# Later-block transposes of a two-layer MLP moved from TensorE to 32x32 transposes on VectorE

## Chip, cores, metric

The kernel runs on one core of one Trainium2 chip. The metric is the device time of one execution in microseconds (us). Before the change it is 411.44 us (median of 4 runs, 411.21 to 412.17). The profile's span leaves out about 1.7 us of that. Engines are named as in the profile: PE is the matmul engine and PEld its weight loads, DVE is VectorE, ACT ScalarE, POOL GpSimd, SP the engine that issues DMAs.

## The reference

```python
B, S, D, F = 1, 2048, 1024, 3584          # all bf16
def reference(x, w1, b1, w2, b2):
    y = _layernorm(x, axis=-1)             # no scale, no shift, eps 1e-5
    h = gelu_tanh(jnp.einsum("bsd,df->bsf", y, w1) + b1)
    return jnp.einsum("bsf,fd->bsd", h, w2) + b2
```

## The kernel before

The 2048 rows are 16 tiles of 128 rows, in four blocks of 512. All weights stay in SBUF. For each block PE computes hT = gelu(w1.T y.T + b1) in 28 groups of 8 matmuls ("first matmul", L509), then the output in 8 groups of 28 matmuls of 512 columns ("second matmul", L527). One output group is 6.04 us of PE.

The first matmul contracts over D, so it needs y transposed, with D on partitions. Each normalized 128x1024 tile is turned by eight PE transposes of 128x128 into PSUM, and another engine copies the result into `yT`. For blocks 1 to 3 these batches of eight stand between the first four output groups of the block before:

```python
def phase2(b):                                   # PE
    for st in range(TPB):
        for dc in range(NDC):
            bank = O_BANKS[n_o % len(O_BANKS)]   # two output banks
            w.wait(s_oe, n_o - len(O_BANKS) + 1) # the bank was evacuated
            for k in range(KF):
                ...                              # 28 matmuls of 512 columns
            ins.then_inc(s_o, 1)
            n_o += 1
            q = st * NDC + dc
            if b + 1 < NB and q < TPB:
                transposes((b + 1) * TPB + q)    # 8 PE transposes of the next block
```

ACT copies those twelve tiles to `yT`, and DVE evacuates the output banks, adding b2:

```python
# ACT, after the gelus of block b
for t in range((b + 1) * TPB, (b + 2) * TPB):
    for ui in tile_units[t]:
        copy_unit(ui)                            # yT <- PSUM, 128x1024

# DVE
for b in range(NB):
    if b + 1 < NB:
        for t in ...: stats_of(t)                # mean and variance
        for t in ...: normalize(t)               # waits for POOL's 1/sqrt of that tile
    evacs(b)                                     # 8 evacuations of 128x512
```

At the start, tile 0's reciprocal root is done on DVE (a chain of dependent one-column instructions) and every other tile's on POOL. The DVE order is: statistics, normalize and copy tile 0; statistics of 1 and of 2; normalize and copy 1; then statistics of 3, tile 2, tile 3. PE's order in block 0 comes from a small planner in the kernel that models when data arrive. It cuts the first groups into narrow pieces of 128, 256 or 384 columns, so that PE can begin with one tile.

Of the kernel before, what the change touches and what calls it, by code (L numbers as in the profile page):

```python
# [11 lines left out]
P = 128  # L12
LN_EPS = 1e-5
# [3 lines left out]
N_WARM = 0  # L17


class _Eng:  # L20
# [5 lines left out]
    def wait(self, sem, val):  # L26
        if val <= 0:
            return
        if self.seen.get(sem.name, 0) >= val:
            return  # L30
        self.seen[sem.name] = val
        self.e.wait_ge(sem, val)
# [15 lines left out]
def _plan_block0(KF, TPB, avail_ft, t_norm, t_pe0, c_tr, c_copy, c_col):  # L48
# [6 lines left out]
    while n_done < KF * TPB:  # L55
        if next_tr < TPB and t_norm[next_tr] <= t:
            ops.append(("T", next_tr))
            t += c_tr
            ready[next_tr] = t + c_copy
            next_tr += 1  # L60
            continue
# [15 lines left out]
        if best is not None:  # L77
            i, j0, j1 = best
            ops.append(("G", i, j0, j1))
            for j in range(j0, j1):  # L80
                done[i][j] = True
            n_done += j1 - j0
            t += c_col * (j1 - j0)
            continue
# [7 lines left out]
def bass_standalone__mixer_channel_mlp__prompt_kernel(nc, x, w1, b1, w2, b2, out):  # L92
# [27 lines left out]
    dma_order = [("x", 0), ("b1", 0), ("x", 1) if TPB > 1 else None]  # L120
    nx = 2
# [6 lines left out]
    while nx < TPB:  # L128
        dma_order.append(("x", nx))
        nx += 1  # L130
# [9 lines left out]
    dma_order = [d for d in dma_order if d is not None]  # L140

    def dma_bytes_rate(kind, idx):
        if kind == "x":
            return P * D * 2, 0.387
        if kind == "b1":
            return F * 2, 0.05
        if kind == "b2":
            return P * D * 2, 0.387
        if kind == "w1":
            a, b = w1_chunks[idx]  # L150
            by = (b - a) * P * D * 2
            desc = (b - a) * P * 2
            return by, (0.290 if desc <= 512 else 0.348 if desc <= 1024 else 0.387)
        a, b = w2_chunks[idx]
        return (b - a) * P * D * 2, 0.387

    t = 2.75
    arrive = {}
    for kind, idx in dma_order:
        by, rate = dma_bytes_rate(kind, idx)  # L160
        t += by / 1024.0 / 1024.0 * 1.048576 / rate / 1000.0 * 1000.0 / 1000.0 if False else by / (rate * 1e6)
        arrive[(kind, idx)] = t + 0.6
    avail_ft = [arrive[("w1", ft_chunk[ft])] for ft in range(KF)]
    DVE_CHAIN_TILES = [0]
    dve_b0 = [("S", 0), ("N", 0), ("C", 0)]
    for j in range(1, TPB):
        dve_b0.append(("S", j))
        if j + 1 < TPB and j == 1:
            dve_b0.append(("S", j + 1))
        if j >= 2 and j + 1 < TPB:  # L170
            dve_b0.append(("S", j + 1))
        dve_b0.append(("N", j))
        dve_b0.append(("C", j))
    seen_ops = set()
    dve_b0 = [o for o in dve_b0 if not (o in seen_ops or seen_ops.add(o))]
    c_stats, c_chain_v, c_chain_p, c_norm, c_tr, c_copy = 1.7, 1.9, 3.2, 0.6, 0.5, 0.8
# [4 lines left out]
    for kind, j in dve_b0:  # L181
        if kind == "S":
            tv = max(tv, arrive[("x", j)]) + c_stats
            if j not in DVE_CHAIN_TILES:
                tp_chain = max(tp_chain, tv) + c_chain_p
                rs_done[j] = tp_chain
        elif kind == "N":
            if j in DVE_CHAIN_TILES:
                tv += c_chain_v
            else:  # L190
                tv = max(tv, rs_done[j])
            tv += c_norm
            t_norm[j] = tv
        else:
            tv = max(tv, t_norm[j] + c_tr) + c_copy
    plan, _t_end = _plan_block0(KF, TPB, avail_ft, t_norm, t_norm[0], c_tr, c_copy, 0.45)
    assert plan[0] == ("T", 0)

    units = [(0, 0, KH, T_BANKS[0], "V"), (0, KH, KD, T_BANKS[1], "V")]
    for tt in range(1, NT):  # L200
        units.append((tt, 0, KD, T_BANKS[len(units) % 2], "V" if tt < TPB else "A"))
    cnt = {"V": 0, "A": 0}
    unit_copy_count = []
    for (_t0, _a, _b, _bank, cp) in units:
        cnt[cp] += 1
        unit_copy_count.append((cp, cnt[cp]))
# [12 lines left out]
    for b in range(1, NB):  # L219
        for ft in range(KF):  # L220
            groups.append((b, ft, 0, SB))
            for j in range(TPB):
                h_need[(b, ft, j)] = len(groups)

    with ExitStack() as es:
# [39 lines left out]
        s_ca = E(nc.semaphore("s_ca"))  # L265
# [8 lines left out]
        s_copy = {"V": s_cv, "A": s_ca}  # L274
# [6 lines left out]
        def _(sp):  # L281
# [14 lines left out]
            n_out = 0  # L296
            for b in range(NB):
                for st in range(TPB):
                    t = b * TPB + st
                    last = (b == NB - 1 and st == TPB - 1)  # L300
                    if not last:
                        w.wait(s_oe, (t + 1) * NDC)
                        sp.dma_start(out[0, t * P:(t + 1) * P, :], x_sb[:, t, :]).then_inc(s_od, 16)
                        n_out += 1
                    else:
                        for dc in range(NDC):
                            w.wait(s_oe, t * NDC + dc + 1)
                            sp.dma_start(out[0, t * P:(t + 1) * P, dc * DC:(dc + 1) * DC],
                                         x_sb[:, t, dc * DC:(dc + 1) * DC]).then_inc(s_od, 16)
                            n_out += 1  # L310
            sp.wait_ge(s_od, 16 * n_out)
# [20 lines left out]

        POOL_CHAIN_TILES = [t for t in range(NT) if t not in DVE_CHAIN_TILES]
        pool_rs_count = {t: i + 1 for i, t in enumerate(POOL_CHAIN_TILES)}
        pool_st_count = {t: i + 1 for i, t in enumerate(POOL_CHAIN_TILES)}

        RSTD_FIN = (NR_ITERS - 1) % 2

        @block.gpsimd
        def _(g):  # L340
# [7 lines left out]
            for t in POOL_CHAIN_TILES:  # L348
                w.wait(s_st, pool_st_count[t])
# [3 lines left out]
        def _(v):  # L353
            w = _Eng(v)
            nv = 0

            def chain(ins):
                nonlocal nv
                nv += 1
                ins.then_inc(s_v, 1)  # L360
                w.wait(s_v, nv)

            n_st = [0]

            def stats_of(t):
# [4 lines left out]
                if t in DVE_CHAIN_TILES:  # L370
                    chain(ins)
                else:
                    ins.then_inc(s_st, 1)
                    n_st[0] += 1
                    assert pool_st_count[t] == n_st[0]

            cnt_v = [0]

            def normalize(t):
                if t in DVE_CHAIN_TILES:  # L380
                    nonlocal nv
                    cnt_v[0] = nv
                    last = rstd_single(v, w, t, s_v, cnt_v)
                    nv = cnt_v[0]
                    chain(last)
                else:
                    w.wait(s_rs, pool_rs_count[t])
                v.tensor_scalar(x_sb[:, t, :], x_sb[:, t, :], mv[:, t, 0:1], ry[:, RSTD_FIN, t:t + 1],  # L388
                                ALU.subtract, ALU.mult).then_inc(s_y, 1)

            def copy_unit(ui):
                t, k0, k1, bank, cp = units[ui]
                assert cp == "V"
                slot = (t // TPB) % NYS
                j = t % TPB
                w.wait(s_tr, ui + 1)
                v.tensor_copy(yT[:, k0:k1, slot * SB + j * P: slot * SB + (j + 1) * P],  # L397
                              ps_t(bank)[:, k0:k1, :]).then_inc(s_cv, 1)

            def copies(t):  # L400
                for ui in tile_units[t]:
                    copy_unit(ui)

            def evacs(b):
                for st in range(TPB):
                    t = b * TPB + st
                    for dc in range(NDC):
                        n_ev = t * NDC + dc
                        bank = O_BANKS[n_ev % len(O_BANKS)]
                        w.wait(s_b2, 16)  # L410
                        w.wait(s_o, n_ev + 1)
                        v.tensor_tensor(x_sb[:, t, dc * DC:(dc + 1) * DC], ps[:, bank, 0:DC],  # L412
                                        b2_bc[:, dc * DC:(dc + 1) * DC], ALU.add).then_inc(s_oe, 1)

            for kind, j in dve_b0:
                if kind == "S":
                    stats_of(j)
                elif kind == "N":
                    normalize(j)
                else:  # L420
                    copies(j)
            for b in range(NB):
                if b + 1 < NB:
                    for t in range((b + 1) * TPB, (b + 2) * TPB):
                        stats_of(t)
                    for t in range((b + 1) * TPB, (b + 2) * TPB):
                        normalize(t)
                evacs(b)

        @block.scalar  # L430
        def _(a):
# [6 lines left out]

            def copy_unit(ui):
                t, k0, k1, bank, cp = units[ui]  # L440
                assert cp == "A"
                slot = (t // TPB) % NYS
                j = t % TPB
                w.wait(s_tr, ui + 1)
                a.activation(yT[:, k0:k1, slot * SB + j * P: slot * SB + (j + 1) * P],  # L445
                             ps_t(bank)[:, k0:k1, :], ACTF.Copy).then_inc(s_ca, 1)

            gi = 0
            for b in range(NB):
                while gi < len(groups) and groups[gi][0] == b:  # L450
# [126 lines left out]
```

## Time and profile before

| part | us | where read |
|---|---|---|
| time, span | 411.44, 409.8 | runs, page |
| PE busy | 397.8 (97%) | page |
| DVE, ACT, POOL busy | 59.1, 94.9, 38.1 | page |
| second matmul of block 0, with transposes | 50.14 | chain of waits |
| the same in the last block, without | 48.36 | chain of waits |
| one batch of 8 PE transposes | 0.45 | chain of waits |

From the page of the kernel before, its first line of busy time, then the shares of the chain that ended last:

```profile
PE 397.8 (97%) x2041; PEld 192.9 (47%) x2041; DVE 59.1 (14%) x110; ACT 94.9 (23%) x142; POOL 38.1 (9%) x142
...
PE 95%; DMA 2%; SPq 1%; DVE 1%; issue 0%
PE ps L527 47%; PE ps L509 46%; PE ps L482 2%; DMA x_sb<-in_x_dram 2%; SPq L292 1%; DVE stats L368 0%; SPq L285 0%; DVE yT L397 0%; DVE x_sb L412 0%; SPq L287 0%; DVE x_sb L388 0%; DVE mv L369 0%
```

The chain is PE's own work: two matmul lines hold 93%, and the transposes (L482) hold 2%. A faster DVE, ACT or POOL would shorten nothing in the middle of this kernel.

The chain of waits in order of time for the same kernel (start, duration, what):

```profile
63.13 6.04 PE ps L527 x28
69.17 0.45 PE ps L482 x8
69.62 6.04 PE ps L527 x28
75.67 0.45 PE ps L482 x8
...
88.64 0.45 PE ps L482 x8
89.09 24.17 PE ps L527 x112
```

Each batch of eight transposes pushes the following output group back by 0.45 us. The last four groups (24.17 us) have none between them.

The start, from the timeline of PE, with the idle time before a piece and what ended it in brackets:

```profile
8.17 1.04 PE L482 MATMUL ps<-ident,x_sb 128*128 128x128 bf16 x8 [4.25 <-DVE x_sb L388]
9.38 5.85 PE L509 MATMUL ps<-yT,w_sb 128*128 128x128 bf16 x64 [0.18 <-DVE yT L397]
15.35 0.62 PE L482 MATMUL ps<-ident,x_sb 128*128 128x128 bf16 x8
```

Tile 0 is transposed at 8.17, eight narrow groups (64 matmuls of 128 columns) run to 15.23, and tile 1 is transposed at 15.35. In this run nothing seems to separate the groups from the transposes. That reading turns out to matter, the more so as the chain of waits of the same profile goes another way there: not through the groups, but through the arrival of tile 2's x, its statistics and the normalization of tile 1, which ends at 15.30.

```profile
6.86 6.33 DMA x_sb<-in_x_dram
...
14.88 0.42 DVE x_sb L388
15.30 0.05 issue
15.35 0.64 PE ps L482 x8
```

The end, from the chain of waits: the last evacuation takes 0.69 us, and the span ends at 409.8, so 2.16 us of store follow.

```profile
406.95 0.69 DVE x_sb L412
```

### The profile page before, as it was taken

The numbers are of one execution on the slowest core, as the hardware profiler recorded it, in microseconds if no ns is written. First come the engines' busy times: TensorE is split into PE (matmuls) and PEld (weight loads), VectorE is DVE, ScalarE is ACT, GpSimd is POOL, SyncE is SP. The second block draws the span as 40 slices with busy tenths as digits, with TensorE's granted clock in tenths as the row PEclk, the third lists the DMA queues.
The fourth block names the chain that finished last, engine by engine and source line by source line (L and its number), as shares of the span: only waits on it lengthen the run. The fifth ranks groups of instructions, "written<-read, shape, count | busy, mean of one in ns | idle before, by whom it ended". The sixth has DMA issues, their size and how long they took to land.

```text
span 409.8 us, 4576 instructions
## 1 busy us (share of the span) xinstructions
PE 397.8 (97%) x2041; PEld 192.9 (47%) x2041; DVE 59.1 (14%) x110; ACT 94.9 (23%) x142; POOL 38.1 (9%) x142
## 2 busy tenths in 40 slices
PE   2999999999999999999999999999999999999997
PEld 1854475454444444444444444445444444444443
DVE  5526100011071000011034000011010000001101
ACT  1434342120034433021004444221002333300000
POOL 0606300000054000000007100000000000000000
PEclk9999999999999999999999999999999999999999
DMA  8999940000000000000000000000000000000000
GB/s 231 346 361 386 387 163 2 27 26 2 26 26 2 0 0 2 0 27 26 26 27 0 2 0 0 2 26 2 26 26 27 0 0 2 0 2 26 26 27 26
DMA packets 18014, 23.63 MB, mean 58 GB/s; under 512 B 843, under 2 KB 10315, under 8 KB 17995
## 3 DMA queue, kind: packets, MB, share of 16 engines
q1 hardware_dynamic: 17994, 23.34, 16.8%
q8 instruction: 16, 0.26, 0.3%
q14 instruction: 4, 0.02, 0.0%
HBM read 19.14 MB, written 4.19 MB: 57 GB/s over the span
## 4 chain that ended last, share of the span: by engine, by line
PE 95%; DMA 2%; SPq 1%; DVE 1%; issue 0%
PE ps L527 47%; PE ps L509 46%; PE ps L482 2%; DMA x_sb<-in_x_dram 2%; SPq L292 1%; DVE stats L368 0%; SPq L285 0%; DVE yT L397 0%; DVE x_sb L412 0%; SPq L287 0%; DVE x_sb L388 0%; DVE mv L369 0%
## 5 line engine op out<-in xcount | busy, mean ns | idle before, releaser
L509 PE MATMUL ps<-yT,w_sb 128*128 128x512 bf16 (+3 forms) x1016 | 197.1, 358 | 1.1 <-DVE yT L397 1.1
L527 PE MATMUL ps<-w_sb,hT 128*128 128x512 bf16 x896 | 196.0, 379 | 0.0
L509 PEld LDWEIGHTS ps<-yT,w_sb 128*128 128x128 bf16 x1016 | 97.6, 100 | 99.5 <-issue 1.7
L527 PEld LDWEIGHTS ps<-w_sb,hT 128*128 128x128 bf16 x896 | 87.1, 98 | 102.6
L454 ACT ACTIVATE hT<-ps,b_sb 128x512 bf16<-128x512 f32 (+3 forms) x127 | 80.9, 637 | 195.1 <-PE ps L509 194.8
L412 DVE TENSOR_TENSOR x_sb<-ps,b_bc 128x512 bf16<-128x512 f32 x32 | 22.1, 691 | 308.6 <-PE ps L527 308.6
L445 ACT ACTIVATE yT<-ps 128x1024 bf16<-128x1024 bf16 x12 | 12.3, 1024 | 66.9 <-PE ps L482 66.9
L368 DVE BATCH_NORM_STATS2 stats<-x_sb 128x6 f32<-128x512 bf16 x32 | 21.7, 678 | 12.1 <-DMA x_sb<-in_x_dram 11.6
L320 POOL TENSOR_SCALAR ve<-mv 128x1 f32<-128x1 f32 x15 | 3.1, 204 | 177.0 <-DVE mv L369 176.1
L482 PE MATMUL ps<-ident,x_sb 128*128 128x128 bf16 x128 | 10.2, 225 | 4.4 <-DVE x_sb L388 4.2
L482 PEld LDWEIGHTS ps<-ident,x_sb 128*128 128x128 bf16 x128 | 8.7, 101 | 7.6 <-DVE x_sb L388 4.6
L388 DVE TENSOR_SCALAR x_sb<-x_sb,mv,ry 128x1024 bf16<-128x1024 bf16 x16 | 8.5, 533 | 22.8 <-POOL ry L327 22.7
L326 POOL TENSOR_SCALAR rb<-ry,gh 128x1 f32<-128x1 f32 x30 | 10.3, 343 | 3.0
L327 POOL TENSOR_SCALAR ry<-rb,ry 128x1 f32<-128x1 f32 x30 | 8.0, 267 | 3.1
L326 POOL TENSOR_SCALAR rb<-yi,gh 128x1 f32<-128x1 f32 x15 | 5.1, 343 | 1.6
L327 POOL TENSOR_SCALAR ry<-rb,yi 128x1 f32<-128x1 f32 x15 | 4.6, 306 | 1.6
L467 PE MATMUL ps<-ident,b_raw 28*128 28x28 bf16 x1 | 0.2, 176 | 3.7 <-DMA b_raw<-in_b_dram 3.7
L321 POOL TENSOR_SCALAR gh<-ve 128x1 f32<-128x1 f32 x15 | 3.4, 227 | 1.3
L397 DVE COPY yT<-ps 128x1024 bf16<-128x1024 bf16 (+1 forms) x5 | 2.9, 585 | 4.1 <-PE ps L482 4.1
L369 DVE BATCH_NORM_AGGREGATE mv<-stats 128x2 f32<-128x12 f32 x16 | 3.3, 209 | 0.5
L322 POOL TENSOR_SCALAR yi<-ve 128x1 int32<-128x1 int32 x15 | 2.9, 192 | 1.2
L467 PEld LDWEIGHTS ps<-ident,b_raw 28*128 28x128 bf16 x1 | 0.1, 99 | 3.7 <-issue 3.7
(17 smaller groups left out, 4.6 us busy)
## 6 DMA issues: line engine op xcount, KB each, us to landing
w_sb<-in_w_dram SPq DMA_DIRECT2D x12, 1024.0 KB, 12.4
x_sb<-in_x_dram SPq DMA_DIRECT2D x16, 256.0 KB, 9.6
out_dram<-x_sb SPq DMA_DIRECT2D x15, 256.0 KB, 2.0
w_sb<-in_w_dram SPq DMA_DIRECT2D x4, 512.0 KB, 6.8
b_bc<-in_b_dram SPq DMA_DIRECT2D x1, 256.0 KB, 12.1
out_dram<-x_sb SPq DMA_DIRECT2D x2, 128.0 KB, 1.7
b_raw<-in_b_dram SPq DMA_DIRECT2D x1, 7.0 KB
```

The costliest lines, as they stand in the source:

```text
L292: sp.dma_start(w1_sb[:, :, a * P:b * P], w1_v[:, :, a * P:b * P]).then_inc(s_w1[idx], 16)
L321: chain(eng.tensor_scalar(gh[:, c], ve[:, c], -0.5, 0.0, ALU.mult, ALU.add))
L326: chain(eng.tensor_scalar(rb[:, c], cur, cur, gh[:, c], ALU.mult, ALU.mult))
L327: last = eng.tensor_scalar(nxt, rb[:, c], 1.5, cur, ALU.add, ALU.mult)
L368: chain(v.bn_stats(stats[:, t, c * 6:(c + 1) * 6], x_sb[:, t, c * BNC:(c + 1) * BNC]))
L388: v.tensor_scalar(x_sb[:, t, :], x_sb[:, t, :], mv[:, t, 0:1], ry[:, RSTD_FIN, t:t + 1], ALU.subtract, ALU.mult).then_inc(s_y, 1)
L412: v.tensor_tensor(x_sb[:, t, dc * DC:(dc + 1) * DC], ps[:, bank, 0:DC], b2_bc[:, dc * DC:(dc + 1) * DC], ALU.add).then_inc(s_oe, 1)
L445: a.activation(yT[:, k0:k1, slot * SB + j * P: slot * SB + (j + 1) * P], ps_t(bank)[:, k0:k1, :], ACTF.Copy).then_inc(s_ca, 1)
L454: a.activation(hT[:, ft, c0:c0 + ncol], ps[:, bank, 0:ncol], ACTF.Gelu_apprx_tanh, bias=b1_sb[:, ft:ft + 1]).then_inc(s_hf, 1)
L482: ins = pe.transpose(ps_t(bank)[:, k, :], x_sb[:, t, k * P:(k + 1) * P], ident[:, :])
L509: ins = pe.matmul(ps[:, bank, 0:ncol], lhsT=w1_sb[:, k, ft * P:(ft + 1) * P], rhs=yT[:, k, slot * SB + c0: slot * SB + c0 + ncol], start=( ...
L527: ins = pe.matmul(ps[:, bank, 0:DC], lhsT=hT[:, k, st * P:(st + 1) * P], rhs=w2_sb[:, k, dc * DC:(dc + 1) * DC], start=(k == 0), stop=(k = ...
```

## The change

The intent is to take the transposes of blocks 1 to 3 off PE. DVE transposes 32x32 blocks from SBUF to SBUF, so 16 instructions of 32 partitions by 256 elements, each writing its blocks to the mirrored place, make a full transpose of one 128x1024 tile, with no PSUM and no copy (run e1_after: 192 of them for the twelve tiles, 0.436 us each, and the result correct). A planner in the kernel, with modelled durations, puts them into DVE's program between the evacuations. Two smaller changes ride along: a new order at the start, and a split of the last output group. The core of the diff, shortened:

```diff
+Q = 32
-    DVE_CHAIN_TILES = [0]
-    dve_b0 = [("S", 0), ("N", 0), ("C", 0)]   # then S1 S2 N1 C1 S3 N2 C2 N3 C3
+    DVE_CHAIN_TILES = [j for j in (0, 1) if j < TPB]
+    # S0 N0 C0 S1 N1 C1 S2 S3 N2 C2 N3 C3; tiles 2 and 3 keep POOL's root
 ...
+    ogroups = []                               # output groups; the last is split
+                if last and DC >= 4 * P:
+                    ogroups.append((b, st, dc * DC, DC - P))
+                    ogroups.append((b, st, dc * DC + DC - P, P))
 ...
+    for n, tg in enumerate(og_time):           # the DVE program of blocks 1 to 3
+        while bi < len(bg):
+            start = max(tv, release(bg[bi]))
+            if start + bg[bi][2] > tg - 0.3:   # would delay evacuation n
+                break
+            dve_prog.append((bg[bi][0], bg[bi][1]))
+            ...
+        dve_prog.append(("E", n))
 ...
+                elif kind == "X":              # DVE, 192 times
+                    t, q, c = arg
+                    src = x_sb[Q * q:Q * (q + 1), t, :].rearrange("p (k c a) -> p k c a", k=KD, c=4)[:, :, c, :]
+                    dst = yT[Q * c:Q * (c + 1), :, col0:col0 + Q]
+                    ins = v.transpose(dst, src)
+                    if q == 3 and c == 3:
+                        ins.then_inc(s_xt, 1)
 ...
-                if b + 1 < NB:                 # ACT: the twelve copies go
-                    for t in range((b + 1) * TPB, (b + 2) * TPB):
-                        for ui in tile_units[t]:
-                            copy_unit(ui)
 ...
-                        if b + 1 < NB and q < TPB:   # PE: 96 transposes go
-                            transposes((b + 1) * TPB + q)
```

The reciprocal roots of blocks 1 to 3 also move from POOL, tile by tile, to one batched chain of four columns per block on DVE.

## The prediction

> **What bounds it now.** TensorE. In the page of the kernel before, PE is busy 397.8 of 409.8 us, at granted clock 1.0. The chain of waits gives PE 95% of the span: L527 (second matmul) 47%, L509 (first) 46%, L482 (transposes) 2%. After 23 us the chain is matmul against matmul with no hole: a block is 48.35 us of first matmul, then 48.35 of second. DVE (59 us), ACT (95) and POOL (38) wait for PE in the table of waits.
>
> **Removed.** 96 PE transposes (12 tiles x 8). Each batch of eight stands in the chain as 0.45 us between two 6.04 us groups. The second matmul of block 0 runs 63.13 to 113.27 = 50.14 us against 48.36 in the last block, which has no transposes: 1.8 us per block, three blocks, 5.35 us, all on the critical path. Twelve ACT copies (1.02 us each, 12.3 in all) and the POOL reciprocal-root chains of blocks 1 to 3 go too, but PE never waited for them after block 0: worth nothing.
>
> **Added.** 192 DVE transposes of 32x256. No such instruction is in this trace. Estimate: BATCH_NORM_STATS2 reads 512 elements per partition in 0.68 us, DVE TENSOR_TENSOR 512 in 0.69; at about one element per ns plus 0.15 us, 256 take about 0.42 us.[...] So 27 us of DVE per block, 81 in all, plus three batched chains of about 2.5 us. DVE rises to about 145 us of 405.
>
> **Does DVE delay PE?** DVE runs in order, so a late transpose delays an evacuation; two output banks mean PE stalls only if an evacuation is a whole group (6 us) late. Tightest is block 1, whose 64 transposes stand before evacuation 0: x tile 4 lands at 29.99, stats 6.2 us, chain 2.5, normalizations 2.3, transposes 27 to 28, ending near 69. Evacuation 0 is due at 69.2 and hurts only after 74.5; that would need over 0.5 us per transpose. In later blocks some 11 transposes (4.8 us) plus an evacuation (0.7) fit in a 6.04 us group. I expect no stall.
>
> **Start.** Tile 1's chain moves from POOL to DVE, tiles 2 and 3 are normalized 0.5 to 2 us later. In the timeline PE does eight narrow groups until 15.23 and transposes tile 1 at 15.35, so an earlier tile 1 gains 0.1 us; later tiles may cost 0.2 to 0.4 in small waits. Net +0.2.
>
> **Tail.** The last group is split 384+128, so the closing evacuation shrinks from 0.69 us to about 0.29 (estimate as above), the final store from 128 to 32 KB. Gain 0.4 to 0.5 us.
>
> **Sum.** 411.44 - 5.35 - 0.45 + 0.2 = 405.8 us (1.4% less). Range 404.9 to 407.3. Over 2% faster 0.03, within 2% 0.94, slower 0.03.
>
> **What would show it.** No L482-like pieces in the chain after block 0; eight second-matmul groups of blocks 0 to 2 back to back in 48.35 us; block pitch 96.7 us against 98.5; DVE transposes of 0.35 to 0.47 us; evacuations of blocks 0 to 2 within 1 us of their group's end, or at least no wait of PE for DVE; last evacuation about 0.3 us; the second matmul of block 0 starting at 63.1 +- 0.5.
>
> **What would make it wrong.** A DVE transpose of 0.6 us or more[...] would stall PE at block 0's second output group by several us and eat the gain; a worse order of narrow groups at the start; matmuls slowed by DVE traffic, shown as more than 0.216 us per matmul.

Two passages are cut above: a second estimate of a DVE transpose, which no trace of this case shows, and a reason in brackets why one might be slow. The forecast's sum came to 405.8 us and loses no term by this, since it has none for DVE. What is left is 0.42 us for one transpose: 26.9 us for the 64 before evacuation 0, which then end at 67.9 us. What the text has above that, up to "28" and "near 69", went with the cut estimate.

The estimate can be checked against the runs. In the profile of before, a one-column TENSOR_SCALAR on DVE takes 0.155 us (L320) and the 128x512 evacuation 0.691 us (L412), so 0.536 us for 511 columns more, 1.05 ns each. The evacuations of the changed kernel lie on that line: 0.29 us for 128 columns and 0.56 for 384. It does not fit every instruction: the normalization of 1024 bf16 columns takes 0.53 us (L388).

## The result

All ratios here are the mean time of one kernel's fast runs over that of the other's fast runs of the same rounds, so they are not quite the ratios of the medians that are quoted beside them.

| | median us | runs | ratio to before (95%) |
|---|---|---|---|
| before | 411.37 | 12, 411.10 to 412.17 | |
| after | 404.93 | 8 of 9 within 404.51 to 405.30 | 0.9842 (0.9832 to 0.9851) |

The change gains 6.4 us, where 5.6 had been forecast. The median lies at the fast edge of the stated range of 404.9 to 407.3. "Within 2%" held. The changed kernel's result is correct.

The ninth run took 1084.99 us, and it is the one that was profiled with the result. Its chain of waits has pieces like this one:

```profile
147.11 133.36 PE ps L571 x224
```

That is 0.595 us per matmul (133.36 / 224) instead of 0.216, over the whole run, with a granted clock of 1.0 in the records, while DVE's transposes took their usual 0.436 us. It was not seen again in the 30 listed runs of the later kernels with DVE transposes. It is not used in any comparison below. Its cause is open.

So the changed kernel was run again for a profile.

> The changed kernel again, for a profile in the fast state (the profiled run that came with the result took 1085 us with every 128x512 matmul at 0.595 us, against 404.5 to 405.3 us in the eight other runs). Main theory: 404.9 us; no transposes in the chain after block 0, second matmul of blocks 0 to 2 in 48.35 us each, that is 5.4 us of the 6.5 us gained; the rest is split between the tail (0.45) and the start (0.6, where I had forecast a loss of 0.2), so the second matmul of block 0 should start at 62.5 rather than 63.1. Rival: the start is as before (63.1) and the rest of 0.6 us lies in the tail or in the blocks.

It measured 405.05 us (4 fast runs, 404.55 to 406.28), ratio 0.9845 (0.9827 to 0.9863). From the page of this profiled run (404.55 us), the busy line, the chain's shares, and the group of DVE transposes (line, engine, shapes, count | busy us, mean ns | idle before):

```profile
PE 389.9 (97%) x1972; PEld 191.1 (47%) x2005; DVE 151.7 (38%) x345; ACT 83.6 (21%) x134; POOL 5.6 (1%) x25
...
PE 95%; SPq 2%; DMA 2%; issue 1%; DVE 0%
...
L482 DVE STREAM_TRANSPOSE yT<-x_sb 32x256 bf16<-32x256 bf16 x192 | 83.6, 436 | 3.0
```

DVE is now busy for 151.7 us, 92.6 more than before, and the chain gives it 0%: none of that work is on the path.

The chain of waits through the second matmul of block 0, to be held against the lines shown of before (the pieces of 49 are cut by missing records, not by waits):

```profile
62.19 10.74 PE ps L571 x49
72.93 0.05 issue
72.98 10.74 PE ps L571 x49
...
105.35 5.13 PE ps L571 x23
110.48 5.61 PE ps L553 x26
```

No transposes are left between the groups: 62.19 to 110.48 is 48.3 us, where it was 50.1.

The start of the same run, from the timeline of PE:

```profile
7.97 1.03 PE L529 MATMUL ps<-ident,x_sb 128*128 128x128 bf16 x8 [4.09 <-DVE x_sb L443]
9.19 4.94 PE L553 MATMUL ps<-yT,w_sb 128*128 128x128 bf16 x64 [0.18 <-DVE yT L449]
13.96 0.61 PE L529 MATMUL ps<-ident,x_sb 128*128 128x128 bf16 x8
```

Tile 1 is transposed at 13.96 instead of 15.35. The start was forecast to lose 0.2 us; this hints that it did not. And the end, from the chain of waits:

```profile
400.67 0.29 DVE x_sb L495
```

The last evacuation takes 0.29 us instead of 0.69, as forecast.

### The profile page after: what moved, and what is told of

Its sections match the earlier page's. It is cut to its first block, busy times and chain, and to the rows that moved or that the text cites. A ratio compares the mean times of both kernels' runs of the same rounds, so it can differ in the third digit from the quotient of the medians.

```text
span 1083.0 us, 4636 instructions
## 1 busy us (share of the span) xinstructions
PE 1072.0 (99%) x2005; PEld 345.1 (32%) x2005; DVE 151.5 (14%) x345; ACT 83.6 (8%) x134; POOL 5.6 (1%) x25
## 4 chain that ended last, share of the span: by engine, by line
PE 99%; DVE 0%; DMA 0%; issue 0%
PE ps L553 49%; PE ps L571 49%; PE ps L529 0%; DMA x_sb<-in_x_dram 0%; DVE stats L423 0%; DVE rb L387 0%; DVE yT L449 0%; DVE ry L388 0%; DVE x_sb L443 0%; DVE x_sb L495 0%; DVE mv L424 0%; DVE gh L382 0%; DVE ve L381 0%; DVE yi L383 0%
## 5 line engine op out<-in xcount | busy, mean ns | idle before, releaser
L553 PE MATMUL ps<-yT,w_sb 128*128 128x512 bf16 (+3 forms) x1048 | 535.0, 748 | 1.0 <-DVE yT L449 0.9
L571 PE MATMUL ps<-w_sb,hT 128*128 128x512 bf16 (+2 forms) x924 | 534.5, 818 | 0.0
L553 PEld LDWEIGHTS ps<-yT,w_sb 128*128 128x128 bf16 x1048 | 179.4, 175 | 354.2 <-issue 337.6
L571 PEld LDWEIGHTS ps<-w_sb,hT 128*128 128x128 bf16 x924 | 161.3, 176 | 372.3 <-issue 371.9
L495 DVE TENSOR_TENSOR x_sb<-ps,b_bc 128x512 bf16<-128x512 f32 (+2 forms) x33 | 22.3, 675 | 892.2 <-PE ps L571 892.2
L482 DVE STREAM_TRANSPOSE yT<-x_sb 32x256 bf16<-32x256 bf16 x192 | 83.7, 436 | 3.0
L529 PE MATMUL ps<-ident,x_sb 128*128 128x128 bf16 x32 | 5.5, 373 | 4.1 <-DVE x_sb L443 4.1
L529 PEld LDWEIGHTS ps<-ident,x_sb 128*128 128x128 bf16 x32 | 4.4, 169 | 5.1 <-DVE x_sb L443 4.2
L387 POOL TENSOR_SCALAR rb<-ry,gh 128x1 f32<-128x1 f32 x4 | 1.4, 342 | 0.4
L388 POOL TENSOR_SCALAR ry<-rb,ry 128x1 f32<-128x1 f32 x4 | 1.1, 267 | 0.4
L437 DVE SCALAR_TENSOR_TENSOR ra<-ry 128x4 f32<-128x4 f32 x6 | 1.0, 162 | 0.2
```

The costliest lines, as they stand in the source:

```text
L387: chain(eng.tensor_scalar(rb[:, c], cur, cur, gh[:, c], ALU.mult, ALU.mult))
L482: ins = v.transpose(dst, src)
L495: v.tensor_tensor(x_sb[:, t, c0:c0 + ncol], ps[:, bank, 0:ncol], b2_bc[:, c0:c0 + ncol], ALU.add).then_inc(s_oe, 1)
L529: ins = pe.transpose(ps_t(bank)[:, k, :], x_sb[:, t, k * P:(k + 1) * P], ident[:, :])
L553: ins = pe.matmul(ps[:, bank, 0:ncol], lhsT=w1_sb[:, k, ft * P:(ft + 1) * P], rhs=yT[:, k, slot * SB + c0: slot * SB + c0 + ncol], start=( ...
L571: ins = pe.matmul(ps[:, bank, 0:ncol], lhsT=hT[:, k, st * P:(st + 1) * P], rhs=w2_sb[:, k, c0:c0 + ncol], start=(k == 0), stop=(k == KF - 1))
```

## The experiments

Three parts were changed at once: transposes, tail, start. The main theory after the result was that the transposes gave what had been forecast, and that the surplus came from the start. The rivals were that moving the transposes had freed more than PE's 0.45 us pieces, or that the tail gave all of the surplus. Each part was run alone on the kernel before.

### Only the transposes

The edit is the changed kernel with start and tail put back:

```diff
-    DVE_CHAIN_TILES = [j for j in (0, 1) if j < TPB]
+    DVE_CHAIN_TILES = [0]
+    dve_b0 = [S0, N0, C0, S1, S2, N1, C1, S3, N2, C2, N3, C3]   # as before
-                if last and DC >= 4 * P:
+                if False:
```

(The planner's constants of block 0 were put back too, so PE's order there is that of the kernel before.)

> Only the transposes of blocks 1 to 3 move to DVE (with their batched chains); start order and tail as before. Main theory: 5.4 us faster than before, 406.0, because PE only loses its twelve pieces of 0.45 us. Rival (moving the transposes also removes hidden waits or refills): 6 us or more faster, 405.3 or less.

It measured 406.13 us, against 411.46 of the kernel before: 5.33 us faster, ratio 0.9867 (0.9851 to 0.9882). The forecast for this part was 5.35. The removed ACT copies (12.3 us of busy time) and the POOL chains are in this run as well, so they added nothing that can be seen.

### Only the tail

```diff
+    def pieces(t):
+        res = [(dc * DC, DC) for dc in range(NDC)]
+        if t == NT - 1:
+            c0, n = res.pop()
+            res += [(c0, n - P), (c0 + n - P, P)]
+        return res
 # matmul groups, evacuations and stores go over pieces(t)
```

> The kernel before with only its last output group split 384+128. Main theory: 0.45 us faster, 410.9 (last evacuation 0.29 instead of 0.69 us, store about the same). Rival (tail gives the whole unforecast rest): 1.1 us faster, 410.3.

It measured 410.72 us: 0.74 faster, ratio 0.9981 (0.9969 to 0.9994). By its interval the gain is 0.2 to 1.3 us, so the time alone does not tell 0.74 from the 0.45 of the main theory. The list of DMA issues shows a part that the theory had left out. First of the kernel before, then of the changed kernel (KB each, us from issue to landing):

```profile
out_dram<-x_sb SPq DMA_DIRECT2D x2, 128.0 KB, 1.7
```

```profile
out_dram<-x_sb SPq DMA_DIRECT2D x1, 96.0 KB, 1.6
out_dram<-x_sb SPq DMA_DIRECT2D x1, 32.0 KB, 1.4
```

The evacuation gives 0.69 - 0.29 = 0.40 us and the smaller store 1.7 - 1.4 = 0.3 us, together 0.7.

### Only the start

```diff
-    DVE_CHAIN_TILES = [0]
+    DVE_CHAIN_TILES = [0, 1]
+    dve_b0 = [S0, N0, C0, S1, N1, C1, S2, S3, N2, C2, N3, C3]
 # on the kernel before; planner constants as in the change
```

> The kernel before with only the new start: tile 1's reciprocal root on DVE, tiles 2 and 3 later, and the PE order that the planner makes of it. Main theory now: 0.6 us faster, 410.8, second matmul of block 0 from 62.5. The prediction's own step: 0.2 us slower, 411.6. Rival (the start does nothing): 411.4.

It measured 410.89 us: 0.57 faster, ratio 0.9982 (0.9969 to 0.9994), that is a gain of 0.2 to 1.3 us. The forecast of a loss of 0.2 is refuted.

The three parts add up to 5.33 + 0.74 + 0.57 = 6.64 us; the whole change measured 411.46 - 405.05 = 6.41 in the same job. They are additive within the spread of the runs.

### Undoing start and tail

The same two parts were taken out of the changed kernel, one at a time.

> The changed kernel with the old start (tile 1's reciprocal root on POOL, statistics of tile 2 ahead of tile 1's normalization). Theory, from the start alone being 0.57 us faster on the old kernel: 0.6 us slower than the changed kernel, 405.5; the transposes of tile 1 start at 15.3 to 15.6[...]. Rival (the parts are not additive; the start is worth nothing here): 404.9.

> The changed kernel without the split of the last group. Theory, from the tail alone being 0.74 us faster on the old kernel (0.40 of it the shorter evacuation, 0.3 the shorter store): 0.7 us slower, 405.6; last evacuation 0.69 us, last store 1.7 instead of 1.4. Rival (the forecast was right and 0.74 was noise): 0.45 slower, 405.35.

They measured 405.65 (ratio 0.9854, 0.9839 to 0.9870) and 405.76 us (ratio 0.9856, 0.9839 to 0.9872), with the kernel before at 411.51 in that job. The changed kernel itself was not in it; against its 405.05 of the other job the losses are 0.6 and 0.7 us, and by the ratios, each taken within its own job (0.9845 for the changed kernel), 0.4 and 0.5 us. These intervals overlap that of the changed kernel, so the times alone would not settle differences this small. The traces do: without the split, the last evacuation is 0.69 us again, and with the old start PE waits for DVE before tile 1. PE's timeline with the old start put back:

```profile
9.21 4.74 PE L547 MATMUL ps<-yT,w_sb 128*128 128x128 bf16 x64 [0.18 <-DVE yT L443]
15.56 0.62 PE L523 MATMUL ps<-ident,x_sb 128*128 128x128 bf16 x8 [1.62 <-DVE x_sb L437]
```

The reason is in DVE's timeline of the same run. The statistics of tile 2 come ahead of tile 1's normalization (L437), and they wait for a DMA:

```profile
13.43 1.42 DVE L417 BATCH_NORM_STATS2 stats<-x_sb 128x6 f32<-128x512 bf16 x2 [2.37 <-DMA x_sb<-in_x_dram]
14.89 0.21 DVE L418 BATCH_NORM_AGGREGATE mv<-stats 128x2 f32<-128x12 f32 x1
15.01 0.49 DVE L437 TENSOR_SCALAR x_sb<-x_sb,mv,ry 128x1024 bf16<-128x1024 bf16 x1
```

### What makes the start vary

All the profiles of kernels without extra work before 8 us, other than that of the run of 1085 us, side by side (us, from PE's timeline). The last two are kernels of a later section, "How much room DVE has", whose extra work begins only after 40 us. The ends of the groups are modelled: where nothing stands between, the next transposes start up to 0.17 us before that end.

| run | start order | eight narrow groups | tile 1 transposed at |
|---|---|---|---|
| before | old | 9.38 to 15.23 | 15.35 |
| only transposes | old | 9.17 to 14.18 | 15.27 |
| only tail | old | 9.19 to 14.55 | 15.63 |
| start undone | old | 9.21 to 13.95 | 15.56 |
| after | new | 9.19 to 14.13 | 13.96 |
| only start | new | 9.24 to 14.96 | 14.80 |
| tail undone | new | 9.13 to 15.09 | 14.93 |
| a quarter more on DVE (e11) | new | 9.16 to 13.90 | 13.90 |
| twice as many on DVE (e12) | new | 9.35 to 15.48 | 15.32 |

With the old order, tile 1 comes at 15.3 to 15.6 whenever the groups end, because it waits for tile 2's DMA and statistics. With the new order it comes as soon as the groups end. The groups themselves take 4.7 to 6.1 us, and where exactly is chance ("after", e11 and e12 have the same program up to 40 us): their matmuls start at 106 ns each (ACT's gelus of two successive groups of eight begin 0.85 us apart) and change within the run to about 56 ns (eight transposes in 0.45 us). The matmul records per us, by the windows, rise from 12 to 22 between 11 and 13 us in the changed kernel, and at 14 us in the kernel before. The first batch of transposes is slow as well: eight took 1.03 or 1.04 us at 8 us, where tile 1's took 0.61 or 0.62. In the five profiles whose windows were read per us (before and the runs e1 to e4), PE becomes busy at 7.95 to 8.17 us, and the first such window with 21 or 22 records begins 4.0 to 6.0 us later. What sets that moment was not shown. The granted clock in these windows reads 1.00 all the while, also where the matmuls start at 106 ns (as it read 1.0 in the run of 1085 us, with 0.595 us per matmul of 512 columns), so the records do not show the clock as the cause. The one profile of the kernel before was one with a late change of rate (15.23), and its PE timeline hid the wait for DVE that the three other profiles of the old order show (PE idle 1.1, 1.1 and 1.6 us before tile 1). Its chain of waits, shown above, had the wait.

Tile 1 comes up to 1.7 us earlier, and not all of it reaches the end. In the changed kernel's timeline the weight loads of the next groups wait for the DMA of w1 until 16.64. The second matmul of block 0 starts at 62.2 to 63.0 with the new order and at 63.0 to 63.5 with the old. The 63.0 of the new order is e12, with the latest change: there tile 1 came at 15.32, as with the old order. So the new start's gain differs from run to run, and 0.57 us is its middle over five runs. Waits for tiles 2 and 3 do not eat into it: in the changed kernel PE has no idle time before their transposes (21.89 and 24.68).

### Warming PE up first

If the slow first matmuls cost time, throw-away matmuls before the data arrive should help, above all with the new order. This edit went into the kernel before, into the start alone, and into the changed kernel, as the candidate to beat both:

```diff
             w.wait(s_id, 1)
+            for i in range(60):
+                pe.matmul(ps[:, O_BANKS[1], 0:P], lhsT=ident[:, :], rhs=ident[:, :],
+                          start=(i == 0), stop=(i == 59))
             w.wait(s_b1, 16)
```

> The kernel before with 60 throw-away 128x128 matmuls on the identity from 1.5 us on, so that PE no longer runs the first eight narrow groups at 106 ns a matmul[...]. Theory (the start is bound by when tile 1 is normalized, and that wait is on x tile 2 in the old order): the eight groups end near 13, the transposes of tile 1 still wait until 15.3; no gain, 411.2 to 411.5. Rival (the slow first groups are what costs): 1 us or more faster, 410.4 or less.

> The kernel before with the new start and the same 60 matmuls. Theory: tile 1 is normalized at 13.9 and PE is free then in every run, so it starts 1.3 us ahead of the old order; gain 0.8 to 1.3 us over the kernel before, 410.2 to 410.7, less if the weights then come too late (a wait of PE for the DMA of w1 of some tenths near 16 us). Rival (the start's gain has nothing to do with tile 1's time): as without the extra matmuls, 410.9.

> The changed kernel with the same 60 matmuls; the candidate for a version that beats both. Theory: PE's eight narrow groups end by 13, transposes of tile 1 at 13.9 as in the best run of the changed kernel (404.5): 404.3 to 404.7, and a smaller spread between runs. Rival (weights bind): no change, 404.9.

They measured 414.24, 412.87 and 405.98 us (6 runs each), against 411.55 for the kernel before in that job. Ratios: 1.0037 (1.0002 to 1.0072), 1.0010 (0.9981 to 1.0040), 0.9854 (0.9822 to 0.9886). All three are worse than expected, and the spread is not smaller. It is wide in this job for the kernel before as well (11 runs, 411.16 to 414.82): two of them took 414.0 and 414.8, with a mean granted clock of 0.996. Warmed, five runs of six took 414.2 or more, at 0.991 to 0.996, and the sixth 411.69 at 1.00. So the state with a fallen clock is not the warm-up's alone, but far more frequent with it on the old kernel. For the changed kernel the interval overlaps that without warm-up (0.9827 to 0.9863): no gain, and no loss that is clear of noise. The kernel before, warmed:

```profile
1.46 5.78 PE L467 MATMUL ps<-ident 128*128 128x128 bf16 x60 [1.46 <-POOL ident L345]
...
12.70 1.07 PE L512 MATMUL ps<-yT,w_sb 128*128 128x128 bf16 x16 [0.67 <-DMA w_sb<-in_w_dram]
15.50 0.62 PE L485 MATMUL ps<-ident,x_sb 128*128 128x128 bf16 x8 [1.74 <-DVE x_sb L388]
```

The eight groups did run fast and ended at 13.8, and tile 1 still waited for DVE until 15.50, as the theory says; with the new order (not shown) it came at 13.71 and 14.33. The same groups at the same time, with PE used before, are no longer slow (the first 48 matmuls took 2.89 us, 60 ns each) although the DMA share from 10 to 15 us is 1.12, where it is 1.11 in the kernel before: in these runs the slow rate goes with PE's own first microseconds of work and not with the data traffic of that time. But PE, now ahead of its data, sat idle in pieces (3.5 us of the 10 from 10 to 20 us, none over 1.74), and the granted clock fell. The table of windows for this run (window, length, busy us and instructions of each engine, granted clock, DMA share, GB/s):

```profile
10.00:15.00 5.00, 3.09 (x52) 2.72 (x49) 2.42 (x6) 2.81 (x8) 2.39 (x9) 1.00 1.12 340
15.00:20.00 5.00, 3.42 (x25) 2.53 (x26) 3.18 (x7) 0.37 (x1) 3.63 (x14) 0.65 1.09 350
20.00:25.00 5.00, 5.00 (x35) 3.63 (x34) 1.05 (x2) 1.60 (x4) 1.40 (x5) 0.67 1.10 348
```

From 15 to 25 us the clock was 0.65 to 0.67: at most 5 x (0.35 + 0.33) = 3.4 us of matmul time lost (less, as PE was idle for 1.6 us of it), which covers the 2.7 us by which this kernel is slower. The two warmed kernels with the new order show 0.73 and 0.92 (e6), and 0.81 and 0.85 (e7), in the last two of these windows. What is shown is that the warm-up moved the work forward into waits, for weights and for tile 1, and that the clock fell in or after them in these three profiles. Which of the waits did it stays open. So no version was found that beats the changed kernel.

The difference between the two warmed versions of the old kernel, 414.24 - 412.87 = 1.4 us in favour of the new order, has the expected sign, but since the clock differs between them it can't be put down to the order alone.

### How much room DVE has

The prediction's other main claim was that DVE's added 84 us cost nothing because they fit. To test where that ends, transposes were repeated into scratch. A first build of this (e8) failed for lack of SBUF: it asked for 24 KB of scratch per partition, and 16 KB were free. With 8 KB it was built and ran (e11).

```diff
+                    if c == 1:        # one in four; the second kernel has: if True
+                        v.transpose(scr[Q * c:Q * (c + 1), j * 4 + q, :, :], src)
                     ins = v.transpose(dst, src)
```

> The changed kernel with one in four of the DVE transposes of blocks 1 to 3 done a second time into scratch (48 of them, 16 per block, 0.45 us each). Theory (DVE has under 5 us to spare before evacuation 0 and PE waits for nothing on DVE until that is used up): evacuation 0 starts at 77 instead of 69.8 us, PE waits 3 to 4 us for it in front of the third output group of block 0, and the later blocks stay inside their slack: 408 to 409 us. Rival (DVE work is free as long as its share of the span is low, here 43%): 404.9.

> The changed kernel with one in four of the DVE transposes of blocks 1 to 3 done a second time into scratch (48 of them, 16 per block, 0.45 us each). Theory (DVE has under 5 us to spare before evacuation 0, and PE waits for nothing on DVE until that is used up): evacuation 0 starts at 77 instead of 69.8 us, PE waits 3 to 4 us for it in front of the third output group of block 0, and the later blocks stay just inside their slack: 408 to 409 us. Rival (DVE work is free as long as its share of the span is low, here 43%): 404.9.

> The same with every DVE transpose done twice (192 more, 86 us of DVE). Theory: evacuation 0 at 98.6 us, PE waits 25 us for it in block 0; in blocks 2 and 3 a group gap holds 22 transposes (9.9 us) plus an evacuation against 6.04 us of matmuls, so DVE paces them and PE waits some 14 and 21 us more: 455 to 470 us, although DVE is still only 51% of the span. Rival (share of DVE decides): within 1 us of 404.9.

With a quarter more, 406.67 us (4 runs, 406.06 to 407.87), ratio 0.9882: 1.6 us slower than the changed kernel. With twice as many, 438.54 us, ratio 1.0650. The rival, that only DVE's share counts, is refuted: DVE is 41% and 49% busy in these runs. The sizes were overestimated. In DVE's timeline of the changed kernel, evacuation 0 is this line:

```profile
69.82 0.69 DVE L495 TENSOR_TENSOR x_sb<-ps,b_bc 128x512 bf16<-128x512 f32 x1
```

PE's timeline, a quarter more:

```profile
62.58 12.25 PE L574 MATMUL ps<-w_sb,hT 128*128 128x512 bf16 x56
75.86 36.43 PE L574 MATMUL ps<-w_sb,hT 128*128 128x512 bf16 x168 [1.03 <-DVE x_sb L498]
```

and twice as many (the view was cut at 115 us, so the second line goes on):

```profile
63.01 12.25 PE L574 MATMUL ps<-w_sb,hT 128*128 128x512 bf16 x56
91.72 23.59 PE L574 MATMUL ps<-w_sb,hT 128*128 128x512 bf16 x98 [16.46 <-DVE x_sb L498]
```

PE stops after exactly two output groups, the number of banks, and waits for evacuation 0. In the changed kernel that evacuation comes at 69.82, some 1.6 us after its group, done at 70.51, and it would be needed at 62.19 + 2 x 6.04 = 74.3. So block 1 had 3.8 us to spare out of some 29 us of transposes. A quarter more used it up and 1.03 us beyond. (Of its 1.6 us, 0.4 is the scatter of the start: its second matmul began at 62.58 and not at 62.19.) I had expected 3 to 4 us because I costed a repetition at 0.45 us. A pair of transposes of the same source took 0.77 us in the doubled kernel, so a repetition cost only about 0.33.

In the doubled kernel PE waits for DVE six times, 26.1 us in all. The loss is 33.5 us. Part of the rest is again the clock, as the windows after the wait of 16.46 us show:

```profile
91.70:98.00 6.30, 6.28 (x19) 2.44 (x20) 5.99 (x12) 0.00 (x0) 0.00 (x0) 0.63 0.10 35
98.00:106.30 8.30, 8.30 (x41) 3.73 (x39) 6.34 (x20) 0.00 (x0) 0.00 (x0) 1.00 0.02 7
```

This long wait of PE was paid twice: once as the wait, once as slow matmuls after it (19 in the first 6.3 us, where 29 fit at 0.216 us). The short ones were not. Two of the other waits in the doubled kernel:

```profile
205.36 6.22 PE L574 MATMUL ps<-w_sb,hT 128*128 128x512 bf16 x28 [1.12 <-DVE x_sb L498]
214.52 7.90 PE L574 MATMUL ps<-w_sb,hT 128*128 128x512 bf16 x28 [2.95 <-DVE x_sb L498]
```

The groups after the waits of 1.12 to 1.34 us took 6.22 us, the usual length of an output group in this view (6.21 in the kernel before). Those after 2.95 and 3.07 us took 7.90 and 7.79. In the other kernel, with its wait of 1.03 us, the mean granted clock of the profiled run is 1.00; in the doubled kernel it is 0.973.

## Why the prediction was wrong, and where it was right

**Right: what bounds the kernel, and the transposes.** They were forecast at 5.35 us from the chain of waits (12 pieces of 0.45 us), and measured alone they gave 5.33.

**Right: copies and POOL chains are worth nothing,** and DVE has room. One DVE transpose was put at 0.42 us; measured are 0.436 us in the trace and 0.45 from one to the next. Evacuation 0 was forecast near 69 and came at 69.8. PE never waited for DVE after block 0. The claim that it would take "over 0.5 us per transpose" to hurt also stands: 29 + 3.8 us of room over 64 transposes is 0.51 us.

**Wrong: the start.** The step that failed is "PE does eight narrow groups until 15.23 and transposes tile 1 at 15.35, so an earlier tile 1 gains 0.1 us; later tiles may cost 0.2 to 0.4". That took the end of the groups in one profile as fixed and as the path. It varies from 13.9 to 15.5 with the moment when PE's matmuls speed up, and the old order makes PE wait for tile 1 (tile 2's DMA and statistics, then the normalization) whenever that moment is early. The chain of waits on hand already went through that path. For a run with as late a change the 0.1 us was about right, as e12 shows; as a forecast for all runs it was not. The new order measured 0.57 us faster where +0.2 had been forecast: an error of 0.8 us, most of the miss. The waits for later tiles, put at 0.2 to 0.4, did not show in the changed kernel's PE timeline.

**Too small: the tail.** The mechanism was right and the term for it, "0.4 to 0.5 us", measured 0.74. The evacuation was right (0.29 us). The term left out the store, which lands 0.3 us sooner at 32 KB than at 128 KB, although the prediction itself names the smaller store.

The corrected sum is 411.46 - 5.33 - 0.74 - 0.57 = 404.8; measured 405.05 in that job and 404.93 in the first.

## What to carry to other kernels

When one engine is the whole chain, work moved off it is worth its pieces in the chain: 5.33 us measured, 5.35 read, although DVE takes 7.2 us for a tile (16 x 0.45) where PE took 0.45. It is free on the other engine only as long as each in-order deadline there holds: here two output banks gave 3.8 us of room while DVE was 38% busy, so count the room at the tightest deadline, not the share. Before a step of a forecast leans on one moment of a profile, ask whether that moment is the same in other runs, most of all in the first microseconds of PE, and whether the chain of waits goes through it. And making an engine faster where it runs ahead of its data can lose: the warmed-up PE of the old kernel idled, in five runs of six its mean clock fell, and it took 414.24 us against 411.55.
